# A gated linear-attention block with two mixing layers: state on 112 partitions, block copies, and a place for every step of the weights

## The chip, the cores and the metric

The kernel runs on one core of a Trainium2 chip. The metric is the device time of one execution in microseconds (us), the median of several runs. TensorE (PE) does the matmuls, VectorE (DVE), ScalarE (ACT) and GpSimd (POOL) the rest; each of them, and each queue that issues DMAs, works through its own instructions in program order.

## What is computed

Inputs are q, k, v and f_logit of shape (4 batches, 8 heads, 768 steps, 48), and the weights U, V, w_ch1, w_ch2, w_theta, w_tok_r, w_tok_i and w_ch. The reference, shortened:

```python
f = 1.0 / (1.0 + np.exp(-f_logit))
for t in range(S):
    state = f[:, :, t, :, None] * state + np.einsum('bhd,bhe->bhde', k[:, :, t], v[:, :, t])
    y[:, :, t] = np.einsum('bhd,bhde->bhe', q[:, :, t], state)
x = y.transpose(0, 2, 1, 3).reshape(B, S, 384)
u = x + (x.transpose(0, 2, 1) @ U @ V).transpose(0, 2, 1)
x = u + np.maximum(u @ w_ch1, 0.0) @ w_ch2
theta = x @ w_theta
y = einsum('ts,bsd->btd', w_tok_r, x * cos(theta)) + einsum('ts,bsd->btd', w_tok_i, x * sin(theta))
u = x + y
out = u + np.maximum(u @ w_ch, 0.0)
```

## The kernel before

Every engine's instruction stream is written out by hand. Python functions emit instructions, and lists of (weight, function) fix the order in which they are emitted. `place(main, timed)` walks through a main list; a timed item with place x is emitted ahead of the first main item whose middle lies at or beyond x times the sum of all weights. `spread` and `merge` give the items of a side list evenly spaced places. So a place fixes a position in each engine's program order, not a time.

**Attention.** Each batch is cut into six chunks of 128 steps. `raw` holds q, k and f of one chunk, with the heads in pairs on partitions 0 to 47 and 64 to 111. For chunk c, `pre_a` makes the sigmoid on ACT, `pre_s` the running product p on DVE (L209) and q times p on POOL (L213), `pre_r` the reciprocals of p for four head pairs on DVE (L220) and k divided by p on POOL (L223). `sc` makes the scores on PE, `mask_` masks them on DVE, `kt` turns k on PE and evicts it on ACT (L257). `kv` adds the chunk to the state: PE forms the products, ACT copies them, POOL adds the old state (L306) and multiplies by the last p (L307). `xx` forms the output from the state and the masked scores; `xt` turns it into `xT`. For each pair, the state is kept as block-diagonal 96 columns in `wst` (112 partitions, 4 pairs, 2, 48), so that one matmul serves both heads. Two such tiles alternate.

**First mixing layers.** `au` and `hT` form the low-rank product; `hT(b, th, k)` adds it to `xT` (DVE, L440) and splits the sum into a high and a low part (ACT L444, POOL). `moe1(b)` has 24 pairs of groups: `w1g(th, f)` is nine matmuls (L477), whose result ACT rectifies into hh (L482) and DVE into the rest hl (L483); `w2g(th, f)` multiplies both by w_ch2 (L493, L496) into three accumulators in PSUM banks A0, A1 and A2, and after the last f of a group DVE adds these to `xT` (L500). In the first and the last batch a group has four f's, otherwise twelve.

**Second mixing layers.** For each batch and chunk of 128 steps there is a unit: `theta` has five parts (prep, tr, mmt, trig, rest: split of x, its transposition L586, the matmul with the angles' range reduction on DVE L602 to L606, the products L619 to L623, and the low part of z on POOL), and `tok` is six groups of matmuls (L646). The parts of theta run two units ahead. `chan` is the last layer (L674, L680).

**Weights.** A weight comes in pieces of 64-bit numbers, and each piece goes through four steps: load (a DMA), scale (two ACT instructions, L863 and L865), join (two DVE instructions, L868 and L871) and store (the high part by ACT L135, the low part by POOL L132). `WPOS` gives each of the first 14 pieces (U, V, and 12 halves of w_ch1 and w_ch2) four places: below 1 in batch 0's attention, from 1 on in batch 0's `moe1`. The 30 later pieces (w_theta, w_ch, 24 token pieces) go through `staged`, in which one step does the scale of piece i+1, the join of i, the store of i-1 and the load of i+3; these steps are spread by `merge` over the last batch's `moe1`, and what is left runs three per unit in batch 0's units.

**Order around the start.** Batch 0's attention is one list with `first_h` (the three `hT(0,0,k)`) at its end; its weights sum to 72,300. PE gets filler matmuls on a constant tile (`keep_warm`). The first six items of batch 1's attention are pulled into it at the places `APOS`; the rest is spread over batch 0's `moe1` by `AKNOT`, and `LN` holds the bounds between which `hT(0,1,k)` are spread. U's four steps in the list before:

```python
WPOS = (
    (0.1339, 0.1374, 0.3041, 0.3499),
```

Of the kernel before, what the change touches and what calls it, by code (L numbers as in the profile page):

```python
# [35 lines left out]
N3 = 20  # L36
CWA = 0.101
M3 = ((0.333, 0.867), (0.3, 0.999))
# [3 lines left out]
    (0.1339, 0.1374, 0.3041, 0.3499),  # L42
    (0.3255, 0.5161, 0.6141, 0.702),
    (0.2264, 0.4338, 0.6498, 0.837),
    (0.4876, 0.6876, 0.8144, 0.8617),
    (0.4987, 0.6487, 0.8825, 0.9325),
    (0.6091, 0.7591, 0.9091, 0.9548),
    (0.5164, 1, 1.02, 1.04),
    (0.3519, 0.8121, 1.021, 1.041),
    (0.7387, 1.138, 1.14, 1.16),  # L50
    (0.839, 1.173, 1.193, 1.213),
    (0.9407, 1.257, 1.29, 1.337),
    (1.05, 1.267, 1.4, 1.44),
    (1.043, 1.46, 1.5, 1.54),
    (1.222, 1.625, 1.662, 1.758),
# [61 lines left out]
def tile_kernel(ctx: ExitStack, tc: tile.TileContext, qkf, v, U, V, w1, w2, wth, wch, wtok, vT, out):  # L117
# [49 lines left out]
    wst = [ap_.tile([PR, NP, 2, D], F32, name=f"wst{i}") for i in range(2)]  # L167
# [23 lines left out]
    def attention(b):  # L191
# [68 lines left out]
        def xx(c):  # L260
# [6 lines left out]
            if c:  # L267
                w = st["W", g]
# [13 lines left out]
            if start:  # L282
                return
# [5 lines left out]
            sub(nc.gpsimd, lo[:, c], xf, f32(hi[:, c]))  # L289

        def kv(c):
            g = b * NCH + c
            t = ps("B1" if not start else "A0", [PR, NP, D])
            k, vt = st["k", g], st["v", g]
            for j in range(NP):
                for q, o in ((0, 0), (1, 64)):
                    h = 2 * j + q
                    mm(out=t[o:o + D, j], lhsT=k[:, j, o:o + D], rhs=vt[:, D * h:D * h + D],
                       start=(j == 0), stop=(j == NP - 1), skip_group_check=True)
# [8 lines left out]
            st["W", g + 1] = w.rearrange("p j a e -> p j (a e)")  # L308
# [155 lines left out]
    def moe1(b):  # L464
# [48 lines left out]
    def weights_2(pool):  # L513
        L = []

        def issue(nm, src, i):
            if i == 0:
                thw[nm] = (pool.tile([128, NK, DM], F32R, name=nm + "hi"), pool.tile([128, NK, DM], F32R, name=nm + "lo"))
            return fetch(nc, pool, src[:, 384 * i:384 * i + 384], [128, 384], nc.sync, "r64", bufs=4)

        def store(nm, i, w):
            hi, lo = thw[nm]
            split(hi[:, i], lo[:, i], w, lo_eng=nc.gpsimd)

        for nm, src in (("th", wth), ("ch", wch)):
            for i in range(NK):
                L.append((lambda nm=nm, src=src, i=i: issue(nm, src, i), lambda w, nm=nm, i=i: store(nm, i, w)))
        return staged(L, 4)

    def staged(L, ahead, delay=1, lag=1):  # L530

        got, out = {}, [(0, lambda i=i: got.update({i: L[i][0]()})) for i in range(min(ahead, len(L)))]

        def step(i):
            if i + 1 < len(L):
                got[i + 1][0]()
            if i < len(L):
                got[i] = got[i][1]()
            if i >= lag:
                L[i - lag][1](got.pop(i - lag))  # L540
            j = i - max(lag, delay) + ahead
            if i >= max(lag, delay) and j < len(L):
                got[j] = L[j][0]()

        out.append((0, lambda: got[0][0]()))
        out += [(1000, lambda i=i: step(i)) for i in range(len(L) + lag)]
        return out

    def tok_weights(pool):
        L = []  # L550
        ring = []

        def issue(n):
            if n == 0:
                ring.extend(pool.tile([128, 384, 2], I32, tag="r64", bufs=4, name="r64") for _ in range(4))
            s, i = divmod(n, 4)
            return fetch(nc, pool, wtok[s, :, 384 * i:384 * i + 384], [128, 384], nc.sync,
                         buf=ring[n % 4].rearrange("p n t -> p (n t)"))

        def store(n, w):  # L560
            s, i = divmod(n, 4)
            if i == 0:
                st["tok", s] = wtile(WMAP[s][0]), wtile(WMAP[s][1])
            hi, lo = st["tok", s]
            sl = slice(384 * i, 384 * i + 384)
            split(hi[:, sl], lo[:, sl], w, lo_eng=nc.gpsimd)

        for n in range(4 * NCH):
            L.append((lambda n=n: issue(n), lambda w, n=n: store(n, w)))
        return staged(L, 4, lag=1)  # L570
# [3 lines left out]
    def theta(pool, b, s):  # L574
# [116 lines left out]
    with tc.manual_schedule():  # L691
# [13 lines left out]
        for t in wst:  # L705
            nc.gpsimd.memset(t, 0.0)
# [62 lines left out]
        for b in range(B - 1):  # L769
# [7 lines left out]
            else:  # L777
# [309 lines left out]
```

## Time and profile before

| | us |
|---|---|
| median of 3 runs | 732.85 |
| lowest, highest | 732.4, 736.12 |
| the profiled execution | 735.42 |
| its span, first to last instruction | 733.6 |

| engine | busy us | share of the span |
|---|---|---|
| PE matmuls | 696.8 | 95% |
| PE weight loads | 655.9 | 89% |
| DVE | 463.2 | 63% |
| POOL | 317.6 | 43% |
| ACT | 290.2 | 40% |

In the rows below, times are from the start of the span. In a timeline, the columns are start, length, engine, line of the kernel, operation, output<-input, shape and count, and in brackets how long the engine had been idle before and what ended that. In a table by stage each engine has its busy time and (x) its instructions; PEclk is the granted TensorE clock as a share of 2.4 GHz.

### The profile page before, as it was taken

The numbers are of one execution on the slowest core, as the hardware profiler recorded it, in microseconds if no ns is written. First come the engines' busy times: TensorE is split into PE (matmuls) and PEld (weight loads), VectorE is DVE, ScalarE is ACT, GpSimd is POOL, SyncE is SP. The second block draws the span as 40 slices with busy tenths as digits, with TensorE's granted clock in tenths as the row PEclk, the third lists the DMA queues.
The fourth block names the chain that finished last, engine by engine and source line by source line (L and its number), as shares of the span: only waits on it lengthen the run. The fifth ranks groups of instructions, "written<-read, shape, count | busy, mean of one in ns | idle before, by whom it ended". The sixth has DMA issues, their size and how long they took to land.

```text
span 733.6 us, 12972 instructions
## 1 busy us (share of the span) xinstructions
PE 696.8 (95%) x5221; PEld 655.9 (89%) x5221; DVE 463.2 (63%) x705; ACT 290.2 (40%) x613; POOL 317.6 (43%) x338
## 2 busy tenths in 40 slices
PE   7988899999999999999999999898899999999996
PEld 6766798999899999899989999898799999999996
DVE  8795778666544545544433578779786569459433
ACT  1577474533332224333323466555442233233211
POOL 5586657542443333342432144335555245336212
PEclk9799899999999999999999999999899999999999
DMA  9795253322122222122000243333000000000102
GB/s 176 172 267 133 68 156 75 55 42 49 44 44 45 44 45 43 45 44 44 2 2 1 87 140 104 102 108 109 0 1 22 33 13 11 33 22 1 44 21 70
DMA packets 17956, 46.14 MB, mean 63 GB/s; under 512 B 2272, under 2 KB 8544, under 8 KB 17888
## 3 DMA queue, kind: packets, MB, share of 16 engines
q1 hardware_dynamic: 15760, 39.13, 21.7%
q10 hardware_dynamic: 2128, 6.10, 3.1%
q8 instruction: 43, 0.70, 0.4%
q14 instruction: 25, 0.20, 0.1%
HBM read 40.50 MB, written 4.72 MB: 62 GB/s over the span
## 4 chain that ended last, share of the span: by engine, by line
PE 39%; DVE 12%; ACT 4%; issue 2%; POOL 2%; DMA 1%; DVEq 0%; POOLq 0%; ACTq 0%
PE ps_A L646 12%; PE ps_A L477 7%; PE ps_B L674 5%; PE ps_A L493 5%; PE ps_B L598 3%; PE ps_A L496 2%; DVE r L606 1%; DVE r L605 1%; DVE kk L603 1%; DVE z L622 1%; DVE z L621 1%; DVE sh L619 1%; DVE r L604 1%; DVE kk L602 1%; DVE r L871 1%
## 5 line engine op out<-in xcount | busy, mean ns | idle before, releaser
L483 DVE SCALAR_TENSOR_TENSOR hl<-ps_A,hh 128x384 fp32r<-128x384 f32 x96 | 53.1, 554 | 151.5 <-ACT hh L482 151.3
L646 PE MATMUL ps_A<-W,zh 128*128 128x384 f32 x576 | 126.1, 340 | 4.2 <-ACT zh L623 3.9
L493 PE MATMUL ps_A<-hh,W 128*128 128x384 f32 x576 | 122.1, 347 | 4.1 <-DVE xT L500 2.9
L477 PE MATMUL ps_A<-uh,W 128*128 128x384 f32 x576 | 121.3, 345 | 1.7 <-ACT uh L444 1.7
L493 PEld LDWEIGHTS ps_A<-hh,W 128*128 128x128 f32 x576 | 100.5, 191 | 8.0 <-ACT r L865 2.9
L646 PEld LDWEIGHTS ps_A<-W,zh 128*128 128x128 f32 x576 | 101.1, 189 | 5.1 <-ACT zh L623 4.5
L477 PEld LDWEIGHTS ps_A<-uh,W 128*128 128x128 f32 x576 | 100.0, 190 | 4.8 <-ACT uh L444 2.5
L482 ACT ACTIVATE hh<-ps_A 128x384 fp32r<-128x384 f32 x96 | 46.9, 489 | 140.0 <-PE ps_A L477 139.1
L132 POOL TENSOR_TENSOR zl<-z,zh 128x768 fp32r<-128x768 f32 x24 | 44.8, 1866 | 102.1 <-ACT zh L623 92.6
L220 DVE RECIPROCAL f<-p 112x128 f32<-112x128 f32 x96 | 87.0, 930 | 0.7
L646 PE MATMUL ps_A<-W,zl 128*128 128x384 f32 x288 | 74.3, 339 | 1.9 <-POOL zl L132 1.9
L132 POOL TENSOR_TENSOR ul<-xT,uh 128x384 fp32r<-128x384 f32 x45 | 49.8, 1115 | 52.9 <-ACT uh L444 35.7
L223 POOL TENSOR_TENSOR raw<-raw,f 112x256 f32<-112x256 f32 x48 | 37.5, 782 | 76.4 <-DVE f L220 61.8
L477 PE MATMUL ps_A<-ul,W 128*128 128x384 f32 x288 | 66.9, 338 | 0.6 <-POOL ul L132 0.6
L496 PE MATMUL ps_A<-hl,W 128*128 128x384 f32 x288 | 66.0, 337 | 0.0
L213 POOL TENSOR_TENSOR raw<-raw,p 112x512 f32<-112x512 f32 x24 | 30.9, 1287 | 66.1 <-DVE p L209 54.1
L646 PEld LDWEIGHTS ps_A<-W,zl 128*128 128x128 f32 x288 | 52.5, 190 | 2.5 <-POOL zl L132 2.5
L477 PEld LDWEIGHTS ps_A<-ul,W 128*128 128x128 f32 x288 | 51.9, 189 | 1.6 <-POOL ul L132 1.6
L496 PEld LDWEIGHTS ps_A<-hl,W 128*128 128x128 f32 x288 | 52.0, 190 | 0.0
L609 ACT ACTIVATE sh<-r 128x384 f32<-128x384 f32 x24 | 12.6, 526 | 85.6 <-DVE r L606 85.6
L132 POOL TENSOR_TENSOR W<-r,W 128x384 fp32r<-128x384 f32 x24 | 27.5, 1148 | 42.0 <-ACT W L135 42.0
L602 DVE TENSOR_SCALAR kk<-ps_B 128x384 f32<-128x384 f32 x24 | 13.3, 554 | 43.7 <-PE ps_B L598 43.7
(161 smaller groups left out, 1255.2 us busy)
## 6 DMA issues: line engine op xcount, KB each, us to landing
raw<-in_qkf_dram SPq DMA_DIRECT2D x41, 288.0 KB, 5.2
r<-in_wtok_dram SPq DMA_DIRECT2D x24, 384.0 KB, 3.2
vt<-in_v_dram SPq DMA_DIRECT2D x24, 192.0 KB, 5.4
out_dram<-o SPq DMA_DIRECT2D x24, 192.0 KB, 1.9
xT<-in_w_dram SPq DMA_DIRECT2D x5, 768.0 KB, 4.8
w<-in_w_dram ACTq DMA_DIRECT2D x4, 768.0 KB, 6.9
w<-in_w_dram SPq DMA_DIRECT2D x2, 768.0 KB, 8.2
raw<-in_qkf_dram ACTq DMA_DIRECT2D x5, 288.0 KB, 5.6
```

The source lines that it names most:

```text
L132: eng.tensor_tensor(out=out_, in0=a, in1=b, op=ALU.subtract)
L213: nc.gpsimd.tensor_tensor(out=x, in0=x, in1=p, op=ALU.mult)
L220: nc.vector.reciprocal(out=f[:, j], in_=p[:, j])
L223: nc.gpsimd.tensor_tensor(out=x, in0=x, in1=f[:, j - 1:j + 1], op=ALU.mult)
L477: mm(out=t, lhsT=w1t(lo, fb)[:, k, 128 * fo:128 * fo + 128], rhs=x[:, k], start=(n == 0), stop=(n == 8))
L482: nc.scalar.activation(out=hh, in_=t, func=ACTF.Relu)
L483: nc.vector.scalar_tensor_tensor(out=hl, in0=t, scalar=0.0, in1=f32(hh), op0=ALU.max, op1=ALU.subtract)
L493: mm(out=st["acc"][k], lhsT=w2t(lo, fb)[:, fo, 128 * k:128 * k + 128], rhs=hh, start=(first_of(f) and lo == 0), stop=False)
L496: mm(out=st["acc"][k], lhsT=w2t(0, fb)[:, fo, 128 * k:128 * k + 128], rhs=hl, start=False, stop=last_of(f))
L598: mm(out=t, lhsT=x[:, k], rhs=w[:, k], start=(n == 0), stop=(n == 8))
L646: mm(out=t, lhsT=z[:, i, 128 * k:128 * k + 128], rhs=w[:, S * i + HT * th:S * i + HT * th + HT], start=(s == 0 and n == 0), stop=(s == NCH ...
L674: mm(out=t, lhsT=w[:, k, 128 * m:128 * m + 128], rhs=x[:, k], start=(n == 0), stop=(n == 8))
```

## The change

1. **State.** A new pair of tiles `kvs` (112 partitions, 4 pairs, 48) holds the state undivided. `kv` makes one ACT copy, one POOL add and one POOL multiply over 112 partitions, where there were two of each over 48. A new function `blocks(c)`, called at the end of `xx(c)`, copies it with two ACT instructions into the diagonal blocks of a single `wst`.
2. **V in two halves.** V's 768 columns become two pieces of 384, so the first list has 15 pieces.
3. **Places.** `WPOS`, `LN`, `AKNOT` and `APOS` get new values. The 30 later pieces lose `staged`; each of their four steps has a place in `NPOS` (below 1 in the last batch's `moe1`, from 1 on in batch 0's six units), and the parts of theta of units 0 and 1 have places in `PPOS`.
4. **Accumulators.** In the last batch every other group of `w2g` accumulates in A5, B0 and A2, and the three are added to `xT` in the order 2, 0, 1. The angles' matmul of units 0 and 1 goes to bank B1 instead of B0.
5. **Start.** The first chunk's DMAs and the memset of `first` are emitted behind the first memset of `raw`; one memset of the state goes.

```diff
+NPOS = (
+    (0.0241, 0.0644, 0.0738, 0.0988),
...
+    (0.9525, 0.9978, 1.008, 1.188),
+    (1.001, 1.002, 1.096, 1.205),
+    (1.047, 1.07, 1.12, 1.412),
...
+)
+PPOS = (0.3588, 0.3882, 0.428, 0.4924, 0.4929, 0.5759, 0.5869, 0.7626, 0.7666, 0.8224, 0.8643)
...
 WPOS = (
-    (0.1339, 0.1374, 0.3041, 0.3499),
-    (0.3255, 0.5161, 0.6141, 0.702),
-    (0.2264, 0.4338, 0.6498, 0.837),
...
+    (0.1827, 0.1862, 0.3967, 0.3987),
+    (0.181, 0.3167, 0.4779, 0.5379),
+    (0.1871, 0.3096, 0.78, 0.782),
+    (0.1954, 0.3485, 0.781, 0.8798),
...
-LN = (0.007404, 0.0274)
-AKNOT = (0.0187, 0.264, 0.4151, 0.6622, 0.8953)
-APOS = (0.8165, 0.9565, 0.9621, 0.999, 0.999, 0.999)
+LN = (0.01438, 0.1137)
+AKNOT = (0.0301, 0.2835, 0.5161, 0.6622, 0.8408)
+APOS = (0.8165, 0.9293, 0.9293, 0.9577, 0.9577, 0.999)
...
-    wst = [ap_.tile([PR, NP, 2, D], F32, name=f"wst{i}") for i in range(2)]
+    kvs = [ap_.tile([PR, NP, D], F32, name=f"kvs{i}") for i in range(2)]
+    wst = ap_.tile([PR, NP, 2, D], F32, name="wst")
...
             sub(nc.gpsimd, lo[:, c], xf, f32(hi[:, c]))
+            if c + 1 < NCH:
+                blocks(c)
...
-            w = wst[g % 2]
+            new, old = kvs[g % 2], kvs[(g + 1) % 2]
+            nc.scalar.activation(out=new, in_=t, func=ACTF.Copy)
+            if c:
+                nc.gpsimd.tensor_tensor(out=new, in0=new, in1=old, op=ALU.add)
+            nc.gpsimd.tensor_tensor(out=new, in0=new, in1=pend[:, g, :, None].to_broadcast([PR, NP, D]), op=ALU.mult)
+
+        def blocks(c):
             for q, o in ((0, 0), (1, 64)):
-                new, old = w[o:o + D, :, q], wst[(g + 1) % 2][o:o + D, :, q]
-                pmb = pend[o:o + D, g, :, None].to_broadcast([D, NP, D])
-                nc.scalar.activation(out=new, in_=t[o:o + D], func=ACTF.Copy)
-                if c:
-                    nc.gpsimd.tensor_tensor(out=new, in0=new, in1=old, op=ALU.add)
-                nc.gpsimd.tensor_tensor(out=new, in0=new, in1=pmb, op=ALU.mult)
+                nc.scalar.activation(out=wst[o:o + D, :, q], in_=kvs[(b * NCH + c) % 2][o:o + D], func=ACTF.Copy)
...
-                st["acc"] = [ps(f"A{k}", [128, HT]) for k in range(NK)]
+                two = b == B - 1 and order.index((th, f)) % 2
+                st["acc"] = [ps(t, [128, HT]) for t in (("A5", "B0", "A2") if two else ("A0", "A1", "A2"))]
...
-                if last_of(f):
+            if last_of(f):
+                for k in (2, 0, 1) if b == B - 1 else range(NK):
...
-            t = ps("B0", [128, DM])
+            t = ps("B0" if (b, s) > (0, 1) else "B1", [128, DM])
...
-        merge(m3[6:], (0.0, 0.0, cw[:4]), (CWA, 0.3, cw[4:]), (*M3[0], pre), (*M3[1], tw[:N3]))
+        timed = [list(zip(PPOS, pre)), []]
+        for fs, at in zip(weights_2(p2), NPOS):
+            for f, x in zip(fs, at):
+                timed[x >= 1.0].append((x % 1.0, f))
+        place(m3[6:], timed[0])
```

## Rows read from the trace of the kernel before

**Rows 1.** The page's first part: busy time, share of the span, instructions.

```profile
PE 696.8 (95%) x5221; PEld 655.9 (89%) x5221; DVE 463.2 (63%) x705; ACT 290.2 (40%) x613; POOL 317.6 (43%) x338
```

**Rows 2.** Table by stage: stretch, length, busy time by engine, clock, DMA.

```profile
0.00:65.00 65.00, 55.78 (x588) 43.09 (x589) 52.23 (x61) 36.41 (x73) 42.45 (x62) 0.92 0.74 181
65.00:84.00 19.00, 14.05 (x66) 11.92 (x65) 15.23 (x22) 9.41 (x19) 9.51 (x9) 0.83 0.62 154
84.00:420.00 336.00, 331.58 (x2893) 311.48 (x2892) 183.60 (x272) 124.63 (x279) 134.07 (x167) 1.00 0.22 48
420.00:485.00 65.00, 60.88 (x337) 58.52 (x335) 50.98 (x87) 40.66 (x87) 29.25 (x25) 0.97 0.41 116
485.00:540.00 55.00, 49.03 (x266) 47.46 (x267) 44.03 (x69) 25.40 (x54) 25.58 (x21) 0.94 0.19 51
...
720.00:733.60 13.60, 7.84 (x46) 7.52 (x44) 3.35 (x6) 0.00 (x0) 0.56 (x1) 0.98 0.27 93
```

**Rows 3.** Timeline of ACT and DVE from 19 to 27 us.

```profile
19.70 0.37 ACT L863 ACTIVATE xT<-xT 128x192 f32<-128x192 f32 x1 [8.41 <-DMA xT<-in_U_dram]
...
20.24 0.52 ACT L257 ACTIVATE ktok<-ps_A 128x448 f32<-128x448 f32 x1
20.66 0.62 ACT L200 ACTIVATE f<-raw 112x512 f32<-112x512 f32 x1
...
21.87 1.23 DVE L209 TENSOR_TENSOR_SCAN p<-f,first 112x512 f32<-112x512 f32 x1 [4.26 <-ACT f L202]
...
26.35 0.54 ACT L257 ACTIVATE ktok<-ps_A 128x448 f32<-128x448 f32 x1 [0.87 <-PE ps_A L255]
```

**Rows 4.** Waits of PE over the span: waiter <- releaser: total us, times, longest.

```profile
PE ps_A L646 <- ACT zh L623: 3.9, 2, 2.4
PE ps_B L438 <- DVE xT L440: 3.2, 2, 2.5
...
PE ps_A L646 <- POOL zl L132: 1.9, 2, 0.9
```

**Rows 5.** Timeline of PE: six L477 matmuls at 79.55 and at 422.57 us.

```profile
79.55 2.29 PE L477 MATMUL ps_A<-uh,W 128*128 128x384 f32 x6
...
422.57 1.20 PE L477 MATMUL ps_A<-uh,W 128*128 128x384 f32 x6
```

**Rows 6.** Timeline around 473 us, and the last evictions before unit 0.

```profile
472.32 0.47 ACT L482 ACTIVATE hh<-ps_A 128x384 fp32r<-128x384 f32 x1
...
473.99 2.26 PE L493 MATMUL ps_A<-hh,W 128*128 128x384 f32 x6 [2.58 <-DVE xT L500]
...
484.63 1.49 DVE L500 TENSOR_TENSOR xT<-ps_A,xT 128x384 f32<-128x384 f32 x3 [0.57 <-PE ps_A L496]
```

**Rows 7.** DMAs issued from 4.3 to 4.4 us: KB each, us to landing.

```profile
raw<-in_qkf_dram SPq DMA_DIRECT2D x1, 288.0 KB, 11.5
```

**Rows 8.** The state's lines: count, ns (min/median/max), first and last start us.

```profile
L304 ACT ACTIVATE wst<-ps_A x10: 309/324/326, 22.2 to 57.7; 48x192 f32<-48x192 f32 x10
...
L306 POOL TENSOR_TENSOR wst<-wst,wst x32: 581/590/1306, 34.0 to 371.9; 48x192 f32<-48x192 f32 x32
...
L307 POOL TENSOR_TENSOR wst<-wst,pend x40: 498/504/1305, 27.4 to 372.6; 48x192 f32<-48x192 f32 x40
```

**Rows 9.** DVE by form, 485 to 540 us; the last row 560 to 600.

```profile
L871 DVE SCALAR_TENSOR_TENSOR r<-r 128x384 int32<-128x384 int32 x9 | 7.4, 818 | 0.3
L868 DVE SCALAR_TENSOR_TENSOR r<-r 128x384 int32<-128x384 int32 x9 | 5.0, 553 | 2.5 <-ACT r L865 2.5
L603 DVE TENSOR_SCALAR kk<-kk 128x384 f32<-128x384 f32 x5 | 4.9, 971 | 0.2
...
L603 DVE TENSOR_SCALAR kk<-kk 128x384 f32<-128x384 f32 x4 | 1.5, 385 | 0.1
```

**Rows 10.** Timeline of PE: transposes that open units 0 and 1.

```profile
486.39 0.49 PE L586 MATMUL ps_B<-ident,xT 128*128 128x128 f32 x3
...
494.55 0.49 PE L586 MATMUL ps_B<-ident,xT 128*128 128x128 f32 x3
```

More of the change, by code (lines that the diff above doesn't have):

```diff
@@ L289, in xx @@
             sub(nc.gpsimd, lo[:, c], xf, f32(hi[:, c]))
+            if c + 1 < NCH:
+                blocks(c)
         def kv(c):
@@ L497, in w2g @@
                    start=False, stop=last_of(f))
-                if last_of(f):
+            if last_of(f):
+                for k in (2, 0, 1) if b == B - 1 else range(NK):
                     u = xT[b][:, k, HT * th:HT * th + HT]
                     nc.vector.tensor_tensor(out=u, in0=st["acc"][k], in1=u, op=ALU.add)
+        order = [(th, o) for o in range(0, NF, span) for th in range(2)]
         todo = [(th, f) for o in range(0, NF, span) for th in range(2) for f in range(o, o + span)]
@@ L513, in weights_2, with issue, dst @@
     def weights_2(pool):
-        L = []
-        def issue(nm, src, i):
+        ring = [pool.tile([128, 768], I32, name=f"r64_{i}") for i in range(4)]
+        def issue(n, src):
+            return fetch(nc, pool, src, [128, 384], nc.sync, buf=ring[n % 4])
+        def dst(nm, i):
+            if nm in ("th", "ch"):
+                if i == 0:
+                    thw[nm] = [pool.tile([128, NK, DM], F32R, name=nm + x) for x in ("hi", "lo")]
+                return [t[:, i] for t in thw[nm]]
@@ L525, in weights_2 @@
[L525 to L537, printed above, removed]
-                got[i] = got[i][1]()
[L539 to L570, printed above, removed]
+            split(*dst(nm, i), w, lo_eng=nc.gpsimd)
@@ new lines, in weights_2, with steps_of, one, load @@
+        tok_ = [(s, i, wtok[s]) for s in range(NCH) for i in range(4)]
+        order = [("th", i, wth) for i in range(NK)] + [("ch", i, wch) for i in range(NK)] + tok_
+        return steps_of([(lambda n=n, src=src, i=i: issue(n, src[:, 384 * i:384 * i + 384]),
+                          lambda w, nm=nm, i=i: store(nm, i, w)) for n, (nm, i, src) in enumerate(order)])
+    def steps_of(L):
+        got = {}
+        def one(i):
+            def load():
+                got[i] = L[i][0]()
+            def join():
+                got[i] = got[i][1]()
+            return load, lambda: got[i][0](), join, lambda: L[i][1](got.pop(i))
+        return [one(i) for i in range(len(L))]
@@ L697, in tile_kernel @@
             nc.gpsimd.memset(r[32:64, 2], 20.0)
-        load_raw(0)
-        for t in first:
-            nc.vector.memset(t, P_FLOOR)
+            if r is raw[0]:
+                load_raw(0)
+                for t in first:
+                    nc.vector.memset(t, P_FLOOR)
         load_raw(1)
@@ L704, in tile_kernel @@
         load_v(1)
-        for t in wst:
-            nc.gpsimd.memset(t, 0.0)
+        nc.gpsimd.memset(wst, 0.0)
         nc.gpsimd.memset(f32(wz), 1.0)
@@ L712, in tile_kernel @@
         ring = x23.rearrange("p b k s -> p (b k s)")
-        pieces = [("U", 0), ("V", 0)] + [(j + i, h) for j in range(3) for h in range(2) for i in (0, 3)]
-        SLOT = (0, 1, 4, 5, 10, 11, 2, 0, 1, 4, 10, 2, 0, 1)
+        pieces = [("U", 0), ("V", 0), ("V", 1)] + [(j + i, h) for j in range(3) for h in range(2) for i in (0, 3)]
+        SLOT = (0, 1, 1, 4, 5, 10, 11, 2, 0, 1, 4, 10, 2, 0, 1)
         def w_issue(n):
```

110 lines of the change are left out of this document (57 added, 53 removed).

## The prediction

> **What bounds the kernel now.** I read the page's busy shares first: TensorE is busy 696.8 of 733.6 us [rows 1], so only time in which it stands still, runs at half clock or does filler can be won. The table by stage [rows 2] says where that is. From 84 to 420 us PE is busy 331.6 of 336: nothing to win. The last 13.6 us (5.8 idle) are the last matmuls' tail, and no edit touches them. What is left is four stretches: the start (0 to 65: DVE busy 52.2, PE 55.8, much of it filler on the constant tile `wz`), 65 to 84 (PE 14.05 of 19, granted clock 0.83), 420 to 485 (PE 60.9 of 65, clock 0.97) and 485 to 540 (PE 49.0 of 55, clock 0.94). Then I read the timeline and the waits in each.
>
> **Start.** ACT issues U's DMA and at once waits for it: 8.41 us, to 19.70. Behind it in ACT's order stand the eviction of the transposed k (20.24) and chunk 2's sigmoid (20.66), so DVE's scan of chunk 2 starts at 21.87 after 4.26 us idle [rows 3]. From there DVE is nearly always busy, so the start is late by those 4.26 us.
>
> **65 to 84.** The three `hT(0,1,k)` stand close together, all in bank B0. Each needs the DVE add of the one before, and DVE is at reciprocals: PE waits 3.2 us in two waits, the longer 2.5 [rows 4]. After that the clock is at its lower level (1.2 GHz): six L477 matmuls take 2.29 us against 1.20 at full clock [rows 5].
>
> **420 to 485.** At 473.99 the second layer's group waits 2.58 us for its accumulators' eviction; the matmuls after it run at half clock (six L493 in 2.26 us) [rows 6].
>
> **485 to 540.** DVE does the angles, the trigonometric products and the joins of token weights, and falls behind: PE waits 3.9 us for zh and 1.9 for zl [rows 4], and the clock falls.
>
> **The change part by part.** The sum is made against the profiled execution: 735.4 us, span 733.6 plus 1.8 around it. That is 2.6 above the median of 732.85; I take the gain off the median.
>
> *(a) The start.* The stage's weights sum to 72,300. U's load moves from 0.1339 (9,681) to 0.1827 (13,209): from ahead of mask 0 to behind k's eviction and chunk 2's sigmoid. These now run when their inputs are there: raw 2's later half is issued just after 4.3 us and lands 11.5 us on, at 15.8 [rows 7]; sigmoid and two short copies end near 16.9; scan 2 can start when DVE is free at 21.87 - 4.26 = 17.6 [rows 3]. Gain at that point 4.26. U's own wait remains: issued near 17.4, it still blocks ACT to about 21, but ahead of less.
> Then ACT becomes the tight one. V's two scales, the first weight piece's scale (0.3485 against 0.4338) and U's store now precede chunk 4's sigmoid: four instructions of 384 elements and two of 768, by the 512-element sigmoid's 0.62 us [rows 3] some 3.6 us, so I let about 3 of the 4.26 be lost at chunk 4. Later DVE wins back: the joins of V's second half and of piece (0,0) go behind mask 4 (0.78), where DVE would stand idle later, and the same pieces leave ACT's end of the stage. I take 3.5 us. Bounds: 0 (ACT eats it all) to 6 (V's store and the scale of piece (4,0) also leave the end of the chain).
> *State on 112 partitions:* per chunk POOL drops one add (0.590) and one multiply (0.504), 1.1 us [rows 8]; 16 chunks drop both and the first of each batch a multiply, 19.5 us of POOL. ACT goes from two copies of 0.324 to one over 112 partitions plus two copies to the blocks. The 112x192 copy isn't in the trace: not below the 48x192 copy's 0.324, not above the 112x512 sigmoid's 0.62 [rows 3, 8]; I take 0.33: the nearest row has as many elements in each partition. So ACT +0.33 per chunk, 6.6 in all, in stages where ACT is busy about 40% [rows 2]: 0 on the path from 84 us on, up to 0.33 per chunk in the start (in the 3.5). The wait that it adds is in the second rival below.
> *V in halves:* the same bytes and elements, some 0.1 us per extra instruction, under 1 us in all; 0 on the path, bound 1.
>
> *(b) 65 to 84.* The hT(0,1,k) go from places 0.0074 to 0.0274 to 0.0144 to 0.1137, so a first-layer group lies between two of them, and three of the four first reciprocals of the next batch move ahead of `first_h`, where DVE idles. Removed: 3.2 us of waiting [rows 4], and half clock: 2.29 - 1.20 = 1.1 on one group of six [rows 5]; by the clock of 0.83 over 19 us [rows 2] 6.5 us ran at the lower level, of which half, 3.2, is lost. 6.4 in all; the join of piece (1,0), twice as long as a 128x384 one (553 + 818 ns [rows 9]), now sits between an hT and its add, so I take 5. Bounds 2 to 6.5.
>
> *(c) 485 to 540.* Of 24 token pieces nine are joined and ten stored in batch 0's units before; now seven and eight, and trig of units 2 and 3 stands behind four and five joins, where it had three and six. A join there costs 553 + 818 ns [rows 9] = 1.4 us, not its undisturbed 1.1. To be in time, zh of unit 3 must be there 24.6 us after unit 0 begins: three units of 494.55 - 486.39 = 8.2 us, by their transposes [rows 10]. DVE's work ahead of it: 1.5 (evictions [rows 6]) + 5 x 1.4 + 2 x 4.5 (angles and products: nine operations between 0.385 and 0.553 [rows 9]) + some 4 of stretching = 21.5; with six joins and more stretching it was 25. So zh comes ahead of PE, and 3.9 + 1.9 = 5.8 us of waits [rows 4] go, with the half clock behind them: clock 0.94 over 55 us is 6.6 us at the lower level, of which half, 3.3, is lost [rows 2]. 9.1 in all; two scales now stand right at their DMA's issue (places 1.001/1.002 and 1.047/1.07) and hold ACT for some 2 us each, of which I let 1 reach PE: 8. Bounds 3 to 9.
> The row shows what a piece does beside its own join: L603 takes 971 ns in this stretch and 385 later, when no piece is converted [rows 9].
> The Trainium skill (SBUF — State Buffer, Who interferes with whom) says why: VectorE and GpSimd share a port pair under an exclusive lock, and the later one is fully blocked. The trace agrees with it. By the rule the two extra pieces make the last hidden stage worse by as much as they relieve the units; this is the third rival.
>
> *(d) 420 to 485.* The second set of accumulators takes away the wait for eviction, but not all of 2.58: the group also needs its own hh, which ACT delivers at 472.32 + 0.47 = 472.8, against 473.99 [rows 6]. So 1.2 us from the banks alone, and the half clock behind (2.26 against the 1.20 of six such matmuls [rows 5, 6]) if the wait gets short. The hh was late because ACT waited for the trigonometric products of unit 1. In the new places mmt1 (0.7626) and trig1 (0.7666) are adjacent, so ACT still waits there, for the 4.5 us of angles and products and its own sines, after which hh comes by my count 0.3 to 1.3 us late. I take 1.5 for the wait, 1.1 for the clock and 1.4 for the smaller waits of this stretch, which has 65 - 60.9 = 4.1 us idle in all [rows 2]: 4. Bounds 0 to 5.
> Order of memsets, one memset of the state less ahead of the filler, mmt0 and mmt1 in bank B1: 0, since the filler or PE's other work hides them; bound 0.5 each way.
>
> Sum: 3.5 + 5 + 8 + 4 = 20.5. From this I take 3.5 for what is late next: with PE 8 us earlier at 84, DVE has less slack in the first hidden stage, and ACT's new order holds up single hh. **Gain 17, forecast 732.85 - 17 = 716 us.**
>
> **Rivals.**
> 1. *ACT takes the start's gain, and half of (b)*: (a) 0, (b) 2.5, (c) 7, (d) 2.5: 12 less 2 = 10, 723 us. For it: scales and copies crowd ahead of chunk 4's sigmoid. Against: ACT is busy only 36.4 of 65 us [rows 2].
> 2. *Slower: ACT's order.* `blocks(c)` makes ACT wait for POOL's multiply, which stands behind the products of chunk c+2; nothing on ACT waited for POOL there before. In chunk 0 the multiply began at 27.4 [rows 8], while ACT evicted the next k at 26.35 [rows 3]. The price is 2 us for each of five chunks, 10 in the start, and the same wait in later batches hits hh. There the known price of a late hh is 2.58 + 1.1 = 3.7 [rows 6]; 15 chunks have such blocks. From three of these on (11) the gain of 20.5 is gone; with five (18.5) the time is 732.85 - 20.5 + 10 + 18.5 = 741 us. Against: from 84 on an item of weight 1,600 lies between kv's end and the copies, and POOL is busy 134 of 336 us there [rows 2].
> 3. *The lock*: the last hidden stage has DVE busy 51.0 of 65 [rows 2]; two pieces more at 1.4 + 0.8 us make it 55.4, hl comes late, (d) is 0 and the units start with a backlog, (c) 4: 3.5 + 5 + 4 - 3.5 = 9, 724 us.
> 4. *All of it holds* (no loss of 3.5, upper bounds of (a), (c)): 24, 709 us.
>
> **How the numbers follow.** Forecast 0.45, rival 1 0.2, rival 2 0.1, rival 3 0.15, rival 4 0.1. A measurement of this kernel can tell about 0.5% (3.7 us) from no change. Faster: the forecast, 1, 3 and 4 less the part of 1 and 3 that ends within 0.5% (0.07): 0.83. Same 0.07, slower 0.1. The range takes in rivals 1, 3 and 4 with their bounds, not 2: 705 to 729.
>
> **What would show it.** Scan 2 near 17.6 us; no wait over 1 us at L438 after the first hT; the first L493 of the last groups without a wait for L500; no zh wait in batch 0's units, and clock 1.00 from 485 on. PE idle from 84 to 420 unchanged at 4 to 5 us. Wrong: ACT idle before the block copies with POOL as the releaser, PE waiting for hh in the middle stages, or a start that ends where it did.

## The result, and the profile after

| | before | changed |
|---|---|---|
| median, us (5 runs each, side by side) | 733.38 | 727.39 |
| profiled execution, span | 735.42, 733.6 | 726.67, 724.9 |

The ratio is 0.9911, 95% interval 0.9885 to 0.9937: about 6 us faster, where 17 were forecast. Between the two profiled executions it is 8.7, since before's lay 2.0 above its median and the changed one's 0.7 below. The forecast's steps are held against these 8.7.

The page's first part of the changed kernel, as in [rows 1]:

```profile
PE 692.3 (96%) x5221; PEld 652.1 (90%) x5221; DVE 459.1 (63%) x707; ACT 298.2 (41%) x638; POOL 293.6 (41%) x302
```

Its table by stage, columns as in [rows 2]:

```profile
0.00:65.00 65.00, 53.27 (x530) 42.07 (x530) 53.38 (x65) 33.85 (x76) 31.69 (x50) 0.87 0.72 174
65.00:84.00 19.00, 17.65 (x134) 14.16 (x135) 11.19 (x17) 13.19 (x25) 11.93 (x10) 1.00 0.70 175
84.00:420.00 336.00, 331.07 (x2883) 311.16 (x2882) 185.27 (x276) 130.88 (x294) 119.26 (x142) 1.00 0.22 48
420.00:485.00 65.00, 61.82 (x356) 60.44 (x355) 51.11 (x91) 42.40 (x91) 30.54 (x26) 1.00 0.43 132
485.00:540.00 55.00, 53.13 (x306) 51.23 (x306) 49.29 (x75) 27.22 (x57) 30.13 (x23) 1.00 0.11 31
```

The clock is now 1.00 in each stage from 65 us on (it was forecast from 485 on; only the last 13.9 us, behind the table, have 0.95). But in the start it fell, from 0.92 to 0.87, and PE is busy 2.5 us less there. The waits of PE over the span answer to [rows 4]:

```profile
PE ps_A L266 <- POOL raw L255: 6.9, 9, 3.3
...
PE ps_A L354 <- ACT xf L312: 3.1, 2, 2.8
...
PE ps_A L531 <- ACT hh L519: 2.7, 2, 2.2
PE ps_A L666 <- POOL zl L163: 1.8, 3, 0.8
PE ps_B L475 <- ACT xT L355: 1.3, 2, 0.6
```

No wait for zh is left, and the wait of `hT` for DVE is gone (L475 is before's L438). The wait for zl, which (c) had counted too, stays at 1.8 us (1.9 before), though from 485 to 540 us it is 1.0. The first three rows are new or grown.

One instruction followed through both timelines tells where the 8.7 us came from. Starts in us:

| instruction | before | changed | difference |
|---|---|---|---|
| scan of chunk 0 | 6.52 | 9.51 | +3.0 |
| scan of chunk 2 | 21.87 | 19.71 | -2.2 |
| eviction xf of chunk 3 (L280, now L312) | 50.02 | 54.77 | +4.8 |
| first matmul of the first layer (L477, now L514) | 70.14 | 74.75 | +4.6 |
| first accumulator eviction (L500, now L539) | 96.60 | 95.68 | -0.9 |
| last hT (L438, now L475) | 406.67 | 406.03 | -0.6 |
| unit 0's first token matmul (L646, now L666) | 485.24 | 481.52 | -3.7 |
| transposes in unit 5 (L586, now L606) | 536.84 | 525.54 | -11.3 |
| transposes in unit 8 | 565.41 | 556.82 | -8.6 |

| step of the prediction | forecast | measured here |
|---|---|---|
| (a) start | +3.5 | **-4.6** |
| (b) 65 to 84 | +5 | +5.5 |
| (d) 420 to 485 | +4 | +3.1 |
| (c) 485 to 540, units 0 to 5 | +8 | +7.6 |
| what is late next | -3.5 | -0.3 (96 to 407) and -2.7 (units 5 to 8) |
| sum | 17 | 8.6 |

All of the miss is in the start. The timeline of ACT and DVE there, in the changed kernel:

```profile
2.31 5.93 ACTq L214 DMA_DIRECT2D raw<-in_qkf_dram  x2
8.36 0.63 ACT L232 ACTIVATE f<-raw 112x512 f32<-112x512 f32 x1 [6.12 <-DMA raw<-in_qkf_dram]
9.51 1.23 DVE L241 TENSOR_TENSOR_SCAN p<-f,first 112x512 f32<-112x512 f32 x1 [2.93 <-ACT f L234]
...
19.71 1.22 DVE L241 TENSOR_TENSOR_SCAN p<-f,first 112x512 f32<-112x512 f32 x1
22.63 0.39 ACT L869 ACTIVATE xT<-xT 128x192 f32<-128x192 f32 x1 [3.08 <-DMA xT<-in_U_dram]
```

ACT stands between the issues of raw 2's half (2.31) and raw 3's (done at 8.24), with the first sigmoid behind them. In the kernel before, the two took from 4.18 to 4.97 and the sigmoid began at 5.02:

```profile
4.18 0.79 ACTq L182 DMA_DIRECT2D raw<-in_qkf_dram  x2
5.02 0.63 ACT L200 ACTIVATE f<-raw 112x512 f32<-112x512 f32 x1 [2.78 <-POOL mask masks.py:66]
```

The programs' instruction streams show why: with the loads emitted in another order, the DMAs are given other semaphores, and raw 3's issue waits for another earlier DMA. In the changed program that semaphore is raised by the larger half of raw 0 that SP issues (192 KB, at 2.1 us, 5.8 us to landing); in the program before it was a 96 KB half of raw 0 from ACT, issued first of all.

```
before   L182 DMA raw_81<-in_qkf_dram 48x1536 [waits DMAHW2_49]
changed  L214 DMA raw_81<-in_qkf_dram 48x1536 [waits DMAHW1_49]
```

Scan 2 is no longer held by U (4.26 us idle in [rows 3], none now), so that mechanism did what was forecast. Then, ACT and PE from 33 to 57 us:

```profile
33.55 0.32 ACTq L214 DMA_DIRECT2D raw<-in_qkf_dram  x1
...
42.60 0.63 ACT L232 ACTIVATE f<-raw 112x512 f32<-112x512 f32 x1 [3.26 <-DMA raw<-in_qkf_dram]
43.91 0.49 ACT L312 ACTIVATE xf<-ps_B 128x384 f32<-128x384 f32 x1 [0.20 <-issue]
50.23 0.95 ACT L869 ACTIVATE xT<-xT 128x768 f32<-128x768 f32 x1 [4.25 <-DMA xT<-in_w_dram]
...
44.46 0.90 PE L354 MATMUL ps_A<-ident,xf 128*128 128x128 f32 x3 [2.84 <-ACT xf L312]
46.25 2.08 PE L266 MATMUL ps_A<-raw 48*128 48x128 f32 x16
...
57.17 1.16 PE L266 MATMUL ps_A<-raw 48*128 48x128 f32 x16
```

Two data waits stand in ACT's order: for raw 5, and for weight piece (1,0), whose scale moved from place 1.0 to 0.6603 although its load takes 14.5 us. PE waits 2.84 us, and then sixteen L266 matmuls take 2.08 us instead of 1.16: after that wait PE runs at its lower level (1.2 GHz; the granted clock is 0.51 from 44.4 to 54.6 us).

### The profile page after: what moved, and what is told of

Its sections match the earlier page's. It is cut to its first block, busy times and chain, and to the rows that moved or that the text cites. A ratio compares the mean times of both kernels' runs of the same rounds, so it can differ in the third digit from the quotient of the medians.

```text
span 724.9 us, 12959 instructions
## 1 busy us (share of the span) xinstructions
PE 692.3 (96%) x5221; PEld 652.1 (90%) x5221; DVE 459.1 (63%) x707; ACT 298.2 (41%) x638; POOL 293.6 (41%) x302
## 4 chain that ended last, share of the span: by engine, by line
PE 32%; DVE 11%; issue 6%; POOL 4%; DMA 3%; ACT 3%; SPq 0%; POOLq 0%; DVEq 0%; ACTq 0%
PE ps_A L666 11%; PE ps_A L514 6%; PE ps_B L694 5%; PE ps_A L531 3%; DMA r<-in_wtok_dram 2%; PE ps_B L618 2%; POOL W L163 2%; PE ps_A L534 2%; DVE r L625 1%; DVE r L626 1%; DVE kk L623 1%; DVE z L641 1%; DVE z L642 1%; DVE xT L672 1%; PE ps_B L309 1%
## 5 line engine op out<-in xcount | busy, mean ns | idle before, releaser
L666 PE MATMUL ps_A<-W,zh 128*128 128x384 f32 x576 | 125.3, 338 | 0.7 <-DVE xT L672 0.7
L531 PE MATMUL ps_A<-hh,W 128*128 128x384 f32 x552 | 118.0, 343 | 3.8 <-ACT hh L519 2.7
L514 PE MATMUL ps_A<-uh,W 128*128 128x384 f32 x576 | 119.8, 342 | 0.9 <-ACT uh L481 0.9
L514 PEld LDWEIGHTS ps_A<-uh,W 128*128 128x128 f32 x576 | 99.3, 188 | 3.5 <-ACT uh L481 1.7
L531 PEld LDWEIGHTS ps_A<-hh,W 128*128 128x128 f32 x552 | 94.8, 188 | 7.8 <-ACT hh L519 3.4
L666 PEld LDWEIGHTS ps_A<-W,zh 128*128 128x128 f32 x576 | 100.5, 188 | 1.1 <-DVE xT L672 1.0
L666 PE MATMUL ps_A<-W,zl 128*128 128x384 f32 x288 | 73.8, 336 | 1.9 <-POOL zl L163 1.8
L514 PE MATMUL ps_A<-ul,W 128*128 128x384 f32 x288 | 66.4, 336 | 0.6 <-POOL ul L163 0.6
L666 PEld LDWEIGHTS ps_A<-W,zl 128*128 128x128 f32 x288 | 51.8, 188 | 3.2 <-POOL zl L163 3.1
L514 PEld LDWEIGHTS ps_A<-ul,W 128*128 128x128 f32 x288 | 51.5, 188 | 1.5 <-POOL ul L163 1.5
L534 PEld LDWEIGHTS ps_A<-hl,W 128*128 128x128 f32 x276 | 49.6, 188 | 0.0
L643 ACT ACTIVATE zh<-z 128x768 fp32r<-128x768 f32 x24 | 20.3, 847 | 45.2 <-DVE z L642 45.2
```

The lines of the kernel that those rows point to most:

```text
L514: mm(out=t, lhsT=w1t(lo, fb)[:, k, 128 * fo:128 * fo + 128], rhs=x[:, k], start=(n == 0), stop=(n == 8))
L531: mm(out=st["acc"][k], lhsT=w2t(lo, fb)[:, fo, 128 * k:128 * k + 128], rhs=hh, start=(first_of(f) and lo == 0), stop=False)
L643: nc.scalar.activation(out=zh, in_=z, func=ACTF.Copy)
L666: mm(out=t, lhsT=z[:, i, 128 * k:128 * k + 128], rhs=w[:, S * i + HT * th:S * i + HT * th + HT], start=(s == 0 and n == 0), stop=(s == NCH ...
```

## The experiments

Theory: the start was lost to data that lands late in ACT's order, not to the amount of work. The first three runs undo one edit each and x4_three all three; y1_control is the changed kernel again. I follow the third hT, the PE matmul that ends the start (the first hT's add, of which the expectations speak, begins within 0.2 us of it). Here it is in the kernel before, the changed one and x4_three:

```profile
68.94 0.34 PE L438 MATMUL ps_A<-vs,as__803 128*128 128x384 f32 x1
73.56 0.34 PE L475 MATMUL ps_A<-vs,as__810 128*128 128x384 f32 x1
65.93 0.34 PE L475 MATMUL ps_A<-vs,as__808 128*128 128x384 f32 x1
```

**The order of the first loads** (x1_order)

```diff
-            if r is raw[0]:
-                load_raw(0)
-                for t in first:
-                    nc.vector.memset(t, P_FLOOR)
+        load_raw(0)
+        for t in first:
+            nc.vector.memset(t, P_FLOOR)
```

> Only the emission order of the first memsets and loads is that of before (all memsets, then load_raw(0), the two `first` memsets, load_raw(1)). Theory A (the start was lost at data that lands late in ACT's order, this being the first place): the first sigmoid starts near 5.0 us again instead of 8.36, scan 0 near 6.5 instead of 9.51, scan 2 near 17 instead of 19.71, and the first hT add comes about 3 us earlier than 73.59; the time falls by 2 to 3 us, less if the later wait for raw 5 eats it. Rival B (the start is bound by ACT's and POOL's work on the state and the block copies): scan 0 moves, the first hT add moves by less than 1 us, the time by less than 1.

Measured: 723.33 us (ratio to before 0.9882, 0.985 to 0.9915); scan 0 at 6.52, scan 2 at 16.72, the third hT at 69.54, 4.0 earlier. ACT's timeline:

```profile
3.88 0.79 ACTq L214 DMA_DIRECT2D raw<-in_qkf_dram  x2
4.72 0.63 ACT L232 ACTIVATE f<-raw 112x512 f32<-112x512 f32 x1 [2.48 <-POOL mask masks.py:66]
```

One edit that I had priced at 0 cost 3 us at scan 0. The 4.0 at the third hT are not these 3 alone: in this profile ACT doesn't wait for piece (1,0) either, whose load took 6.6 us here, but PE waits 2.2 us for xf at 24 us and runs near its lower level behind that (granted clock 0.56 from 30 to 38 us), and ACT waits 2.7 us for piece (0,0).

**Two places of weight pieces** (x2_piece40, x3_scale10)

```diff
-    (0.5308, 1.15, 1.155, 1.246),      # x2: (4,0)
+    (0.62, 1.15, 1.155, 1.246),
-    (0.5164, 0.6603, 1.02, 1.059),     # x3: (1,0)
+    (0.5164, 1, 1.02, 1.059),
```

> Only the load of weight piece (4,0) is issued later, place 0.62 for 0.5308, so that its 768 KB no longer stand between the two halves of raw 5 (31.66 on SP, 33.55 on ACT). Theory A: raw 5's second half lands near 39 instead of 42.6, chunk 5's sigmoid does not wait, PE's 2.84 us wait at L354 and the half clock behind it (44.5 to 54.6) go: the first hT add comes 4 to 6 us earlier than 73.59, the time falls by 3 to 5 us. Rival C (the queues are full of the ACT-side pieces anyway): the sigmoid still waits until after 41.5, the time stays within 1 us. Rival B: the wait goes, but the start ends where it did, within 1 us.

> Only the scale of weight piece (1,0) goes back to place 1.0 (end of the stage) from 0.6603. Theory A: ACT's wait of 4.25 us for that DMA (to 50.23) goes and so do two ops of 0.9 us there, but PE is then still at half clock until 54.6, so the first hT add moves by 0 to 1.5 us and the time by 0 to 1.5 us. Rival D (this DMA wait is what makes the start late): the first hT add comes 3 us or more earlier.

Measured: 722.33 (0.9866, 0.9844 to 0.9888) and 722.26 (0.9855, 0.9832 to 0.9878), the third hT at 68.55 and 69.40. For x3 I was wrong: its hT comes 4.2 us earlier, rival D's answer. Its profile also had raw 5 in time (ACT waits 0.6 us for it), with issues at the same times as in the changed kernel, so the control was needed.

**The changed kernel once more** (y1_control)

> The changed kernel itself once more, as a control for the experiment on (1,0)'s scale, whose profile had raw 5's second half land at 39.9 with the issues at the same times. Theory A (raw 5 lands late in the changed kernel each time): time 726 to 729 us again, chunk 5's sigmoid at 42 or later, first hT add near 73.6. Rival E (the landing of raw 5 varies from run to run, and the profile of the changed kernel caught a bad one): sigmoid 5 near 40, first hT add near 69, time 721 to 724.

Measured: 725.92 us (724.15 to 727.34), the third hT at 74.08. The waits of ACT up to 76 us:

```profile
ACT f L232 <- DMA raw<-in_qkf_dram: 7.7, 2, 5.9
ACT xT L869 <- DMA xT<-in_w_dram: 4.6, 1, 4.6
...
ACT wst L345 <- POOL kvs L340: 3.0, 2, 2.1
```

Theory A fell in one point: raw 5 lands at 42.6 in one run and by 39.65 in another, and the time doesn't care. What both profiles share is the wait for piece (1,0), 4.25 and 4.6 us. x3 takes it away by asking later; in x2, where (4,0)'s 768 KB no longer go ahead of it, it is 1.1 us. So x2 and x3 cure one cause, the early scale. By the lower of the two times of the changed kernel, 725.92, they are worth 3.6 and 3.7 us.

**All three edits** (x4_three)

> All three edits together. Theory A: 3 + 4 to 6 + up to 1.5: first hT add near 65 to 67, before the 68.97 of the kernel before; the time falls by 6 to 9 us against the changed kernel, to 718 to 721. Rival B: first hT add not ahead of 71, the time falls by less than 3.

Measured: 717.87 us (0.9794, 0.9774 to 0.9814), the third hT at 65.93. That is 3.0 ahead of before, where (a) had said 3.5, and 8 to 9.5 us under the changed kernel. It is also 2.6 and 3.5 us ahead of x2_piece40 and x3_scale10 at the third hT: about that much the order of the loads is worth where (1,0) is waited for no more. What PE still waits for between 28 and 66 us:

```profile
PE ps_A L334 <- ACT ktok L289: 2.1, 1, 2.1
PE ps_A L354 <- ACT xf L312: 0.2, 1, 0.2
```

**U back in its old place** (y4_uback, on x4_three)

```diff
-    (0.1827, 0.1862, 0.3967, 0.3987),
+    (0.1339, 0.1374, 0.3967, 0.3987),
```

> The kernel with the three edits, and U's load and scale back at places 0.1339 and 0.1374, ahead of mask 0. Theory A (U's wait in ACT's order holds k's eviction and chunk 2's sigmoid, 4.26 us in the kernel before): scan 2 near 21 instead of 16.72, first hT add 3 to 4.5 us later than 65.95, time 720.5 to 722.5. Rival G (the time goes to the late data in any case): scan 2 moves, first hT add moves by under 1.5 us, time 717 to 719.5.

Measured: 721.52 us (0.9824, 0.9792 to 0.9856): 3.7 more. Scan 2 at 21.20, the third hT at 69.89, 4.0 later, and ACT again waits for U:

```profile
ACT xT L868 <- DMA xT<-in_U_dram: 8.0, 1, 8.0
```

The prediction's mechanism for U holds in the profile once the other two causes are out of the way, and its size (4.26, of which 3.5 stay) agrees. The times alone don't settle it: the two intervals overlap, and two of the six runs (717.48 and 718.39) are as fast as x4_three's.

**The state alone, and without it** (y3_state on the kernel before; z4_changed_nostate and z1_nostate with before's state on the changed kernel and on x4_three)

```diff
...
+            nc.scalar.activation(out=new, in_=t, func=ACTF.Copy)
...
+                nc.scalar.activation(out=wst[o:o + D, :, q], in_=kvs[(b * NCH + c) % 2][o:o + D], func=ACTF.Copy)
...
-                nc.scalar.activation(out=new, in_=t[o:o + D], func=ACTF.Copy)
...
```

> The kernel before with the state change alone (112 partitions, block copies on ACT, one block tile). Theory A: the state is free on the path as predicted: first hT add within 1 us of 68.97, time 732 to 735. Rival B (ACT waits for POOL ahead of the block copies and evictions come late, as in the prediction's second rival): ACT waits of 1 to 2 us at the block copies of several chunks, first hT add 2 to 5 us later, time 735 to 739. A gain (POOL has 19.5 us less to do): 729 to 731.

Measured: 741.2 us (1.0098, 1.0068 to 1.0128), slower by 7.8, the first matmul of the first layer at 75.56 instead of 70.14. Timeline of POOL, ACT and PE (L309 multiplies, L314 copies blocks):

```profile
25.56 0.51 POOL L309 TENSOR_TENSOR kvs<-kvs,pend 112x192 f32<-112x192 f32 x1
26.10 0.36 ACT L314 ACTIVATE wst<-kvs 48x192 f32<-48x192 f32 x1 [3.93 <-POOL kvs L309]
...
54.65 0.73 ACT L314 ACTIVATE wst<-kvs 48x192 f32<-48x192 f32 x2 [2.68 <-POOL kvs L309]
57.60 1.09 PE L303 MATMUL ps_A<-vt,ktok 128*64 128x48 f32 x16 [2.87 <-ACT ktok L258]
```

This is the wait of the prediction's second rival, at two chunks: POOL's multiply stands behind later products, ACT waits for it, the next k is evicted late, PE waits 2.87. The start loses 5.4 us; where the other 2.4 of the 7.8 go wasn't looked into. Does the state cost as much in the new order?

> The changed kernel with the state of the kernel before, all else as changed. Theory H: the state took part of what the start lost (ACT waits 2.6 to 3.0 us at two block copies); first hT add 2 to 5 us ahead of 73.56, time 721 to 724. Rival J (the late scale of piece (1,0) sets the start in the changed kernel, whatever the state): first hT add within 1.5 us of 73.56, time 725 to 728.

> The kernel with the three edits, but with the state of the kernel before (two block tiles, ACT copies from PSUM, POOL adds and multiplies on both halves). Alone on the kernel before, the state change cost 7.8 us. Theory H (it costs in the new order too: ACT waits 1.1 us at the block copies of chunk 2, and has one copy more per chunk): first hT add 1 to 4 us ahead of 65.93, time 713 to 716.5. Rival I (in the new order ACT has slack, since U's wait is out of the way, and POOL's 19.5 us count): first hT add within 1 us of 65.93 or later, time 717 to 721.

Measured: 725.55 (0.9887, 0.9856 to 0.9918), as the changed kernel, with piece (1,0) still waited for 4.7 us; and 720.43 (0.98, 0.977 to 0.983), 2.6 more than x4_three, though the runs spread from 717.03 to 724.34. So in the new order no cost of the state shows in the times, as rivals J and I had it, as far as the spread lets one say. The profiles leave room for some: z4_changed_nostate has its third hT at 71.89, 1.7 us ahead of the changed kernel and 2.2 ahead of its control, which is between the ranges of theory H and rival J.

**The accumulators, and the old hT places** (z2_oneacc, z3_hT, each on x4_three)

```diff
-                two = b == B - 1 and order.index((th, f)) % 2
-                st["acc"] = [ps(t, [128, HT]) for t in (("A5", "B0", "A2") if two else ("A0", "A1", "A2"))]
+                st["acc"] = [ps(f"A{k}", [128, HT]) for k in range(NK)]
-LN = (0.01438, 0.1137)
+LN = (0.007404, 0.0274)
-APOS = (0.8165, 0.9293, 0.9293, 0.9577, 0.9577, 0.999)
+APOS = (0.8165, 0.9565, 0.9621, 0.999, 0.999, 0.999)
```

> The kernel with the three edits and one set of accumulators, as before the change. By step (d) of the prediction the banks alone are worth 1.2 us at the last group, with half clock behind it: waits of L531 for L539 of 1 to 2.6 us return between 420 and 485, time 1 to 3 us more than 717.87. Rival K (the group waits for its own hh in any case): no new wait of over 0.7 us, time within 1 us.

> The kernel with the three edits, and LN and APOS as before the change: the three hT(0,1,k) close together again and the reciprocals of the next batch in their old places. By step (b): PE waits at L475 for L477 of 2 to 3.5 us in all return between 66 and 84, with the granted clock of that stretch under 0.9; time 4 to 6.5 us more than 717.87. Rival L (only the earlier end of the start's data, or the DMA's absence, cures this stretch): waits under 1 us, clock 1.00, time within 2 us.

z2_oneacc: 720.81 us (0.9826, 0.9781 to 0.9871; 717.02 to 725.78). Its start was 1.8 later in the profile, so I compare the stretch: from the last hT to the first token matmul 78.8 us with one set, 76.4 with two, 2.4 for the second set. By the times alone it could be nothing, since the two intervals overlap. The waits in its PE timeline:

```profile
436.92 1.33 PE L530 MATMUL ps_A<-hh,W 128*128 128x384 f32 x6 [1.58 <-DVE xT L538]
451.89 1.35 PE L530 MATMUL ps_A<-hh,W 128*128 128x384 f32 x6 [1.85 <-DVE xT L538]
468.17 1.33 PE L530 MATMUL ps_A<-hh,W 128*128 128x384 f32 x6 [1.92 <-ACT r L869]
```

With two sets the last group still waits 1.78 for its own hh (2.16 in the changed kernel), as (d) had said, only longer than its 0.3 to 1.3.

z3_hT: 727.11 us (0.9906, 0.9874 to 0.9938). In its profile the first L514 starts at 67.01 (67.12 in x4_three) and the scan of chunk 1 of the next batch at 81.18 (75.86): 5.4 us lost in between. By the medians it is 9.2 us, but the profiled run is one of the two fastest; what the others lose besides isn't shown. In the profile the clock is 0.91 from 65 to 84 us, and PE's waits equal [rows 4] to the tenth:

```profile
PE ps_B L475 <- DVE xT L477: 3.2, 2, 2.5
```

**U asked for early, waited for late; scales far from their loads** (v1_uearly and v2_slack on x4_three; y2_scale31, also on x4_three, moves only the (3,1) scale)

```diff
-    (0.1827, 0.1862, 0.3967, 0.3987),   # v1, v2
+    (0.1339, 0.1862, 0.3967, 0.3987),
-    (0.1954, 0.3485, 0.781, 0.8798),    # v2
+    (0.1954, 0.4606, 0.781, 0.8798),
-    (0.3106, 0.4606, 0.8355, 0.9329),   # v2
+    (0.3106, 0.62, 0.8355, 0.9329),
-    (0.5676, 0.7591, 0.9091, 0.9916),   # v2, y2
+    (0.5676, 0.86, 0.9091, 0.9916),
```

> The kernel with the three edits, and the scale of piece (3,1) at place 0.86 instead of 0.7591. In the three-edit kernel ACT waits 2.92 us for that DMA (to 48.07), PE waits 2.13 for ktok behind it, and PE is at half clock from 50.3 to 55. Theory A: the waits and the half clock go, first hT add 2 to 4 us ahead of 65.95, time 714 to 716.5. Rival F (DVE's joins, busy without a gap from 42 to 56, bind there): first hT add moves by under 1 us, time 717 to 718.5.

> The kernel with the three edits, with U's load issued early again (place 0.1339) but its scale left late (0.1862), so that the same data is asked for some 5 us earlier and waited for at the same place. Theory M (in the start ACT's order is held wherever a scale stands nearer to its load than the DMA takes): ACT's wait for U falls from 4.2 to about 0.5 us, the following instructions come up to 3 us earlier, first hT add 1 to 3 us ahead of 65.93, time 714.5 to 717. Rival N (U queues behind the raw loads and lands at the same time, near 20, whenever it is asked for): wait above 3 us, time 717 to 719.

> As the former, and four scales of weights at later places, so that none stands within 10 us of its load: (0,0) from 0.3485 to 0.4606, (0,1) from 0.4606 to 0.62, (3,1) from 0.7591 to 0.86. Theory M: no ACT wait of over 1 us for a DMA of weights in the start, no PE wait of over 1 us between 28 and 66, and no half clock there; runs of one kernel agree within 3 us instead of the 10 of the kernel with (3,1) late (714.67 to 725.3); time 711 to 715. Rival F (DVE's joins bind after 42 us): first hT add not ahead of 64.5, time 716 to 719.

y2_scale31: 717.19 us (0.9762, 0.9733 to 0.979), but from 714.67 to 725.3, and its profile shows the long end: another piece's data, (0,0), lands at 29.35 where x4_three had it by 26.39, and U's store behind it makes PE wait; then sixteen L266 take 2.08 us again.

```profile
29.35 0.92 ACT L868 ACTIVATE w<-w 128x768 f32<-128x768 f32 x1 [2.48 <-DMA w<-in_w_dram]
...
31.57 0.83 PE L457 MATMUL ps_A<-xf,u 128*32 128x384 f32 x2 [1.44 <-ACT u L753]
...
35.14 2.08 PE L266 MATMUL ps_A<-raw 48*128 48x128 f32 x16
```

v1_uearly: 716.11 us (0.9765, 0.9728 to 0.9801; 714.0 to 721.02), the fastest median of all; ACT waits 2.2 us for U instead of 4.2, the third hT comes at 62.58. v2_slack: 718.3 (715.88 to 719.71). ACT waits for no weight but U (2.8 us), the spread is 3.8 us, and the third hT comes at 63.20, no earlier than in v1_uearly. So the waits for the other weights are gone, as theory M said, but its further gain isn't there. Nor is the spread explained: v2_slack's runs lie closer together than y2_scale31's and v1_uearly's, but x4_three's, with the scales still near their loads, lie within 2.0 us. Why v2_slack isn't faster than v1_uearly, I can't tell from one profile each; the two intervals overlap.

**The 2.7 us after unit 5** (v3_uldve, on x4_three)

```diff
-                split(..., lo_eng=nc.gpsimd)
+                split(..., lo_eng=nc.gpsimd if b else nc.vector)
```

> The kernel with the three edits, with the six low parts `ul` of batch 0's channel input computed on DVE instead of POOL. Between 540 and 565 the changed kernel lost 2.6 us against before, with DVE busy without a gap and single operations of 0.36 to 0.56 us taking 1.1 to 1.7 beside POOL's products. Theory P (POOL's six products of 1.14 us, beside which DVE's operations stretch, make that loss): the stretch gets no longer, 0 to 2 us are won, time 716 to 718. Rival Q (DVE's own work is the bound; six times some 0.5 us more on it): 2 to 3 us are lost, time 720 to 721.

Measured: 725.1 us (0.9886, 0.9854 to 0.9918), 7 more. PE waits for DVE behind unit 6's transposes, which begin at 522.60:

```profile
531.57 1.65 PE L666 MATMUL ps_A<-W,zh 128*128 128x384 f32 x4 [2.27 <-DVE xT L672]
```

That is rival Q, and more: DVE's own work binds there. From unit 5's transposes to unit 8's this profile takes 35.9 us, x4_three's 31.3, so 4.6 us are lost there; the profiled run is the fastest of the five, and what the others lose besides isn't shown. The changed kernel takes 31.3 us for the same units, the kernel before 28.6. PE's waits there in the changed kernel:

```profile
539.62 0.96 PE L666 MATMUL ps_A<-W,zh 128*128 128x384 f32 x4 [0.68 <-DVE xT L672]
543.43 0.62 PE L666 MATMUL ps_A<-W,zl 128*128 128x384 f32 x2 [0.77 <-POOL zl L163]
549.42 0.79 PE L694 MATMUL ps_B<-uh,chhi 128*128 128x384 f32 x3 [1.37 <-ACT x2tok L608]
```

Together they are 2.8 us, against 0.7 in the kernel before. The last is at two removes DVE's too: on ACT x2tok stands behind zh, and zh waited 1.88 us for DVE's z. DVE works there from 527 to 555 us with single gaps of at most 0.6. That a lighter DVE would win the 2.7 us back is argued, not shown.

## Why the prediction was wrong

The failed step is **(a), the start: forecast +3.5 with bounds 0 to 6, measured -4.6**. One of its terms was priced at nothing, one was left out. Undoing both wins back 7.6 of these 8.1 us at the third hT.

- "Order of memsets ...: 0, since the filler or PE's other work hides them; bound 0.5 each way." I looked for the engine that executes a memset, and not for the DMA issues that change their semaphores with it. The price was 3.0 us at scan 0 (x1_order) and some 3 at the third hT (2.6 and 3.5, x4_three against x2_piece40 and x3_scale10).
- In (a) I weighed the scales that move ahead of chunk 4's sigmoid by their work alone (some 3.6 us, of which 3 to be lost), and the scale of (1,0), which moves ahead of chunk 3's output, not at all. A scale also waits for its DMA, and ACT stands meanwhile; in (c) I had priced just that for two scales. The trace of before had the price: ACT stood 8.4 us for U [rows 3], raw 2's half took 11.5 us [rows 7], and (1,0)'s own load took 13.2 (row below). The cost was some 4 us (x2_piece40, x3_scale10). Against rival 1 I held that "ACT is busy only 36.4 of 65 us"; that says nothing about an engine that stands in a wait with work behind it. How much of the loss belongs to which of the two isn't exact, since x1_order, too, ran without (1,0)'s wait; and up to 2.2 us of the changed start may be the state's (z4_changed_nostate).

The loads to xT that ACT issues from 36 to 37.5 us in the kernel before, with KB and us to landing, are one, that of (1,0):

```profile
xT<-in_w_dram ACTq DMA_DIRECT2D x1, 768.0 KB, 13.2
```

With both out of the way the start ends 3.0 us earlier than before and the kernel takes 717.87 us, 1.9 from the forecast (x4_three); U's share is 3.7, or 4.0 at the third hT (y4_uback).

The other steps held, as their trace signs say: no wait over 1 us at hT (b; undone, 5.4 us come back); no wait for zh and clock 1.00 from 485 on (c); the first L531 of the last groups waits 0.69 for its accumulators and the last one 2.16 for hh instead (d; the set is worth 2.4, of which I had given 1.2 to the banks); PE idle from 84 to 420 us 4.9, as said. "What is late next" was -3.5 and came to -3.0, though not where I put it: only 0.3 from 96 to 407, and 2.7 in units 5 to 8, where PE waits 2.8 us for DVE and for what stands behind it. Rival 3 didn't come: from 420 to 485 us DVE is busy 51.1 us, not 55.4, and (d) gave 3.1. No run undoes (c) alone, nor V's two halves; their part rests on the two profiles.

The state's "0 on the path" agrees with the times in the changed kernel's order (z4_changed_nostate, z1_nostate), but only there: alone it costs 7.8 us (y3_state). Rival 2 named that wait, and its estimate of 10 us for the start stands against 5.4. I gave it 0.1 for reasons that concern the stretch from 84 us on, when the start was where it bites.

## What to carry to other kernels

Price an edit of a program order by the waits it puts into each in-order queue, DMA issues included: for every load, the distance from issue to first use against the longest landing in the trace. An engine with 40% busy time is no buffer when it stands in a wait. And a part that shows no cost in one order can cost 8 us in another, so test parts in the order in which they are to run.

## What the runs showed of the hardware

- A DMA issue that waits for an earlier DMA holds the engine that issues it: ACT stood from 2.3 to 8.2 us, while the two parts of raw 0 that its sigmoid reads had landed by 4.5 us. The Trainium skill (DMA: Bandwidth & Descriptors, Anatomy of one DMA, in a section on DMAs that GpSimd issues) says that DMA engines don't wait on semaphores, the issuing sequencer does, ahead of dispatch; the trace agrees for ACT's queue.
- The same program's loads land up to 3 us apart from run to run (raw 5 at 42.6 and by 39.65 in the changed kernel). In y2_scale31's slowest run a load that landed late put PE into a wait and then at the lower level (granted clock 0.50 from 33 to 44 us). Its runs go from 714.67 to 725.3 us; that the landings make this whole spread isn't shown.
